# Paired PSUM copies, a later load behind the output weights, and semaphores that make GpSimd wait for VectorE: one change to a fused attention and feed-forward kernel

## The chip, the cores and the metric

The kernel runs on one core of a Trainium2 chip. The metric is the device time of one execution in microseconds (us). Each measured run comes with the mean clock that the throttle granted to TensorE, as a share of full speed. One of the first runs of the kernel before, 280.04 us, was slow and is left out.

Engines have short names in the traces: PE is TensorE, PEld its weight loads, DVE is VectorE, ACT is ScalarE, POOL is GpSimd, SP is SyncE.

## The reference

Attention with a causal local band of 96 keys, 8 global keys and a linear distance bias, over 4 batches, 8 heads, 768 positions and head size 64; then RMS norm and a SwiGLU feed-forward layer on the 3072 resulting rows.

```python
scores = scale * np.matmul(q, k.transpose(0, 1, 3, 2)) + bias      # kept: global or local keys only
a = softmax(scores);  x = np.matmul(a, v)                          # (4, 8, 768, 64) -> (3072, 512)
xn = x / np.sqrt(np.mean(x * x, axis=-1, keepdims=True) + 1e-06) * rms_g
g = xn @ w_gate;  val = xn @ w_val                                 # 512 -> 1536
out = (g * sigmoid(g) * val) @ w_out                               # 1536 -> 512
```

## The kernel before

The work is cut into 8 chunks of 384 rows (half a batch each). A chunk goes through transposes of q and k on TensorE (chunks 0 to 2; later ones use DMA transposes), scores, exponential on ScalarE, masks on VectorE and GpSimd, the product with v, the norm, and then 12 pairs of gate and value products and an output product. TensorE works on the feed-forward part of one chunk while the attention of the next is prepared. So the first feed-forward product of chunk 1 needs, ahead of it, the output product of chunk 0, the norm of chunk 1 and the transposes of chunk 2 that have been placed there.

The order of instructions on each engine comes from a planner in the kernel file. It lists operations with an estimated duration and dependences, simulates the engines, and searches 200 random shifts of priority for the shortest plan. That is why any change of a duration or a dependence gives a new order everywhere.

```python
def tr(c, p, name):                       # transposes of one pair of heads into PSUM
    t = ps_m.tile([128, HB, 128], BF16, tag="m", name="trp")
    ...
def cp(c, p, name, eng):                  # and its copy to SBUF, 128 x 384
    copy(eng)(T[name, c][:, p]..., T["tr", c, p, name]...)

def load_w(what, s):                      # 3 parts each of w_gate, w_val, w_out, issued by GpSimd
    nc.gpsimd.dma_start(w_out[:, ds(4 * s, 4), :], ...)

def glob_v(b, lo, hi):                    # "global copy": values of the 8 global keys, 8 x 1040
    nc.vector.tensor_copy(VG[b % 2][0:NG, lo - 1:hi - 1], _brd(V1[b % 2][0:NG, 0], 1, hi - lo))

def rstd(c):                              # the norm's power, on GpSimd
    nc.gpsimd.tensor_tensor(r, T["ssq", c], half_c, op=ALU.pow)

def fu(c, f):                             # u, on VectorE: its end frees a PSUM bank of the gate product
    nc.vector.scalar_tensor_tensor(u, T["t", c, f], 1.0, T["g", c, f][:, 0:CH], ...)

def kg(c, eng):                           # kG: k again with the 8 global keys put into each block
    copy(eng)(t[:, 0:n], k[:, 0:n])
    ...
def gate(what):                           # a tiny GpSimd copy that makes a later load wait
    ...
    elif what == "v2":                    # v of chunk 2 waits for the last w_val
        src, dst = w_val[0:1, 0, DF - 1:DF], t[0:1, 0, 0:1]
# cut: scores, exponentials, masks, norm, feed-forward, planner, the list of operations
```

The softmax here doesn't subtract the row's maximum and nothing guards it: scores larger than these inputs give would overflow.

Of the kernel before, what the change touches and what calls it, by code (L numbers as in the profile page):

```python
# [39 lines left out]
class _Plan:  # L40
# [11 lines left out]
    START = {"SP": 0.7, "ACT": 0.7, "POOL": 1.9}  # L52
    LAG = {"PE": 0.2, "ACT": 0.1, "DVE": 0.1, "POOL": 0.12, "SP": 0.0}

    def __init__(self, sizes, free):
        self.sizes = sizes
        self.order, self.ops = {}, []
        self.first = dict(free)

# [25 lines left out]
    def _start(self, o, eng):  # L85

        t = max(0.8 if o.kb and eng == "ACT" else self.free[eng], o.at[eng])
        if self._shares(o, eng):
            t = max(t, self.port + (0.15 if eng == "DVE" and self.holder == "POOL" else 0.0))
        if o.kb and eng == "POOL" and len(self.sent) >= 8:  # L90
            t = max(t, self.sent[-8].done)
        need = {}
        for b in o.take:
            need[b.ring] = need.get(b.ring, 0) + 1
        for r, k in need.items():
            used, size = self.rings[r], self.sizes[r]
            if r not in self.LOOSE and any(b not in self.queue[r][:k] for b in o.take if b.ring == r):
                return None
            for i in range(len(used), len(used) + k):
                if i >= size:  # L100
                    old = used[i - size]
                    if old.left:
                        return None
                    t = max(t, old.free)
        return t
# [41 lines left out]
    def search(self, tries, keys, spread):  # L147

        rnd, best, shift = random.Random(6), math.inf, {}
        groups = sorted({key for o in self.ops for key in keys(o)}, key=str)  # L150
        for k in range(tries):
            new = dict(shift)
            if k:
                part = rnd.choice((0.05, 0.2, 1.0))
                amp = rnd.choice(spread)
                for g in groups:
                    if rnd.random() < part:
                        new[g] = new.get(g, 0.0) + rnd.uniform(-amp, amp)
            for o in self.ops:
                o.shift = sum(new.get(g, 0.0) for g in keys(o))  # L160
            end = self.run(call=False)
            if end <= best:
                best, shift = end, new
        for o in self.ops:
            o.shift = sum(shift.get(g, 0.0) for g in keys(o))
        self.run()

    def run(self, slack=0.08, call=True):
# [4 lines left out]
        self.port, self.holder, self.sent, self.issue = 0.0, None, [], 0.0  # L173
# [13 lines left out]
        while left:  # L187
# [25 lines left out]
            if o.kb and eng == "POOL":  # L213
                self.issue = t + dur
            elif eng == "DVE" and t < self.issue and o.fn.__name__ in self.SLOW:
                dur += 0.2
# [24 lines left out]
            if call:  # L241
                o.fn(*o.args, *([] if o.only else [eng]))
# [4 lines left out]
def kernel(  # L247
# [77 lines left out]
    def load_heads(c, name):  # L325

        t = cast_tile(c, name).rearrange("x (h i d) -> x h i d", h=H, i=HB)
        src = {"q": q, "k": k}[name][c // 2, :, ds(CH * (c % 2), CH)]
        nc.gpsimd.dma_start(t.rearrange("x h i d -> x h (i d)"), src.rearrange("h (x i) d -> x h (i d)", i=HB))
# [20 lines left out]
    def load_w(what, s):  # L350
        if what == "o":
            nc.gpsimd.dma_start(w_out[:, ds(4 * s, 4), :],
                                moe_w_out[ds(512 * s, 512)].rearrange("(f p) c -> p f c", p=128))
        else:
            src, t = (moe_w_gate, w_gate) if what == "g" else (moe_w_val, w_val)
            nc.gpsimd.dma_start(t[:, :, ds(512 * s, 512)],
                                src[:, ds(512 * s, 512)].rearrange("(c p) f -> p c f", p=128))
# [99 lines left out]
    def tr(c, p, name):  # L457
        t = ps_m.tile([128, HB, 128], BF16, tag="m", name="trp")
        src = T[name + "b", c]
        for i in range(HB):  # L460
            if c == 0:
                nc.tensor.transpose(t[:, i], src[:, ds(DM * i + 128 * p, 128)], ident)
                continue
            for h in range(2):
                nc.tensor.transpose(t[ds(64 * h, 64), i], src[:, ds(D * (HB * (2 * p + h) + i), D)], ident)  # L465
        T["tr", c, p, name] = t

    def cp(c, p, name, eng):
        if (name, c) not in T:
            T[name, c] = qkp.tile([128, HP, CH], BF16, tag=f"{name}T", name=f"{name}T", bufs=2)  # L470
        copy(eng)(T[name, c][:, p].rearrange("x (t i) -> x t i", i=HB),
                  T["tr", c, p, name].rearrange("x i t -> x t i"))

    def cast_block(c, name, i):
        t = cast_tile(c, name)[:, ds(DM * i, DM)].rearrange("x (h d) -> x h d", h=H)
        nc.gpsimd.tensor_copy(t, T["s" + name, c, i])  # L476
# [13 lines left out]
    def cast_v(c, i, eng="POOL"):  # L490
        b, half = divmod(c, 2)
        J = HB * half + i
        copy(eng)(V1[b % 2][:, J, :, 0:D], T["sv", c, i])  # L493

    def copy_vg(c, i, eng="POOL"):
        b, half = divmod(c, 2)
        J = HB * half + i
        copy(eng)(VG[b % 2][:, J - 1], V1[b % 2][:, J])

    def glob_v(b, lo, hi):  # L500
        nc.vector.tensor_copy(VG[b % 2][0:NG, lo - 1:hi - 1], _brd(V1[b % 2][0:NG, 0], 1, hi - lo))  # L501
# [43 lines left out]
    def kg(c, eng):  # L545
        half = c % 2
        n = HB - half
        t = kg_tile(c)
        k = T["k", c].rearrange("x g (i t) -> x i g t", t=128) if c < NE else T["k", c]
        copy(eng)(t[:, 0:n], k[:, 0:n])  # L550
        lo = 1 - half
        copy(eng)(t[:, lo:n, :, 0:NG], _brd(kg_tile(c - half)[:, 0, :, 0:NG], 1, n - lo))

    def mask(c, p, d, eng):
        half = c % 2
        P = T["P", c, p, d]
        if d == 0:
            m = m00[:, ds(2 * p, 2)] if half == 0 else _brd(_brd(md0, 1, HB), 1, 2)
            nc.vector.tensor_tensor(P, P, m, op=ALU.mult)
        else:  # L560
            lo = 1 if half == 0 else 0
            tt = nc.vector.tensor_tensor if eng == "DVE" else nc.gpsimd.tensor_tensor
            tt(P[:, :, lo:HB, :], P[:, :, lo:HB, :],  # L563
# [45 lines left out]
    def rstd(c):  # L609
        r = xp.tile([128, HB], F32, tag="r", name="r")  # L610
        if c >= NX:
            nc.gpsimd.tensor_scalar(T["ssq", c], T["ssq", c], 1e-6, None, op0=ALU.add)
        nc.gpsimd.tensor_tensor(r, T["ssq", c], half_c, op=ALU.pow)
        T["r", c] = r

    def xn(c, i, eng="DVE"):
# [3 lines left out]
        if c >= NX:  # L620
            e = nc.vector if eng == "DVE" else nc.gpsimd
            e.scalar_tensor_tensor(o, x, r, grow, op0=ALU.mult, op1=ALU.mult)
        elif eng == "ACT":
            nc.scalar.activation(o, x, AF.Copy, scale=r)  # L624
        else:
            nc.vector.tensor_scalar(o, x, r, None, op0=ALU.mult)
# [73 lines left out]
    def gate(what):  # L700
# [5 lines left out]
        elif what == "v2":  # L706
            t = T["gate", 2, "v"] = stg.tile([128, H, D], F32, tag="sv", name="sv")
            src, dst = w_val[0:1, 0, DF - 1:DF], t[0:1, 0, 0:1]
# [3 lines left out]
        nc.gpsimd.tensor_copy(dst, src)  # L712
# [32 lines left out]
    def weights(what, s, due, deps):  # L745
        w_ops[what, s] = add("POOL", 0.8, due, load_w, what, s, deps=deps, kb=2.53, packet=96)
# [3 lines left out]
    def early_part(c):  # L750
# [8 lines left out]
        def load_v():  # L759
            for i in range(HB):  # L760
                sb = buf("sv")
                if c == 2 and i == 0:
                    gated.append(add("POOL", 0.15, START, gate, "v2", deps=[w_ops["v", 2]], take=[sb]))
# [39 lines left out]
        glob[c] = add("DVE", 0.41, due, glob_v, b, lo, hi, deps=gs + old)  # L803
        kg_due = due
        for p in range(HP):
            v_ops[p] = vs + [glob[c]] + old
            due = (START + 8 * p, S1 + 2 * p, S2 + 4 * p)[c]
            for name, ops in (("q", q_ops), ("k", k_ops)):
                t = buf("m")
                o = add("PE", (0.42, 0.36, 0.2)[c], due, tr, c, p, name, deps=[ld[name, p][0], const_ops["ident"]] + hold.get(c, []),  # L810
                        take=[t], give=[ld[name, p][1]])
                tk = [] if p else [(qT_buf if name == "q" else kT_buf)[c]]
                ops[c, p] = [add({"ACT": 0.5} if c == 1 else {"ACT": 0.5, "DVE": 0.5}, 0, due + 1, cp, c, p, name, deps=[o],
                                 give=[t], take=tk)]
        if c >= NK:
            kG_buf[c] = buf("kG", HP + 1 + HP)
            o = add({"DVE": 0.56, "POOL": 1.05}, 0, kg_due + 2, kg, c, deps=[x for p in range(HP) for x in k_ops[c, p]],
                    take=[kG_buf[c]], give=[kT_buf[c]])
# [4 lines left out]
    def sequence_part(c):  # L823
# [44 lines left out]
        glob[c] = add("DVE", 0.35, a0 - 1, glob_v, b, lo, hi, deps=gs)  # L868
# [4 lines left out]
    def attention(c, q_ops, k_ops, v_ops):  # L873
# [6 lines left out]
        for p in range(HP):  # L880
# [3 lines left out]
            if c:  # L884
# [4 lines left out]
                else:  # L889
                    kgd, kgb = [kg_ops[c, p]], [kG_buf[c]]  # L890
                    if half:
                        kgd, kgb = kgd + [kg_ops[c - 1, p]], kgb + [kG_buf[c - 1]]
                o = add("PE", 0.58 if c >= NK else 0.75, a + 2, qk, c, p, 2, take=bufs[0] + bufs[1],
# [27 lines left out]
            o = add("PE", 0.4 if c else 0.57, a + 7, av, c, p, deps=masks + v_ops[p], take=[ab], give=Ps)  # L921
# [20 lines left out]
        if c < NX:  # L942
            t = [buf("m", 2), buf("m", 2)]
            if c == 0:
                pad = add("PE", 1.75, a + 3.9, idle, c, deps=norms, take=t)
            o = [add("PE", 0.25, a + 4, xtr, c, i, deps=[x[i]] + ([pad] if c == 0 else []), take=[] if i or c == 0 else t, give=[xnb])
# [62 lines left out]
    load_g = add("SP", 0.5, START - 40, load_grow, kb=0.7, packet=40, deps=[seq_ops["ld", 1, "v", HB - 1]])  # L1009
    for _ in attention(1, *parts[1]):  # L1010
        pass
    for c in range(2, NCH):
        ops = early_part(c) if c < NE else sequence_part(c)
        for _ in attention(c, *ops):
# [12 lines left out]

    plan.search(TRIES, keys, (1.0, 3.0, 8.0))
# [34 lines left out]
```

## Time and profile before

| | kernel before |
|---|---|
| fast runs of the first rounds | 254.01, 253.53, 253.81 us |
| the profiled run | 251.78 us, clock 1.000, span in the trace 250.0 us |
| first feed-forward product of chunk 0 / of chunk 1 | 26.12 / 55.84 us |
| TensorE's last product ends | 246.29 us |

From the profile page of the kernel before: the line of busy times (engine, busy us, share, instructions), and the load of the output weights (queue, count, size of one, median us from issue to landing).

```profile
PE 232.5 (93%) x1952; PEld 133.2 (53%) x1952; DVE 182.5 (73%) x392; ACT 154.4 (62%) x359; POOL 109.1 (44%) x143
...
w_out<-in_moe_w_out_dram POOLq DMA_DIRECT2D x3, 512.0 KB, 20.7
```

TensorE works almost all the time, so only its idle time can be won. A transfer of output weights takes 20.7 us to land. From 26.1 to 56 us the DMA engines move 204 GB/s at a share of 1.24; at that rate its 512 KB alone would take 2.6 us, so by this estimate most of the 20.7 us is the time of other data. What TensorE waited for, in the same kernel (engine, line and instruction, what it waited for; total us, times, longest):

```profile
PE trp L462 <- DVE qb L333: 8.7, 4, 6.7
...
PE xtp L633 <- DVE xn L626: 1.1, 1, 1.1
PE trp L465 <- DMA kb<-in_k_dram: 0.3, 1, 0.3
```

The first line is mostly the start, before there is any data. The left-out line is the wait of 2.4 us that the prediction shows in its timeline.

### The profile page before, as it was taken

To read this page: it belongs to the slowest core of one execution; us is meant where nothing else is said; L and a number is where in the kernel's file an instruction comes from. 1 tells how busy PE (TensorE), PEld (TensorE's weight loads), DVE (VectorE), ACT (ScalarE), POOL (GpSimd) and SP (SyncE) were. 2 spreads that over 40 slices of the span, in tenths; PEclk is the share of its full clock that TensorE was granted. 3 is DMA by queue.
4 is the path that set the end of the run, shared out by engine and by line. 5 is a ranking of instruction groups with operands and counts; after the bars stand their busy time and mean duration, and the time that the engine had idled before them with its cause. 6 is when DMAs were issued, how large, how long until landed. Compare 5 with 4: busy or idle time off the path is not lost.

```text
span 250.0 us, 5245 instructions
## 1 busy us (share of the span) xinstructions
PE 232.5 (93%) x1952; PEld 133.2 (53%) x1952; DVE 182.5 (73%) x392; ACT 154.4 (62%) x359; POOL 109.1 (44%) x143
## 2 busy tenths in 40 slices
PE   0688879989999999999999999999999999999993
PEld 0346445645555555655655655565555555555541
DVE  6796598878796878998698859887976787545700
ACT  7787746977869879866863695548753444323321
POOL 4094942368939947735576468334420010000000
PEclk9999999999999999999999999999999999999999
DMA  6999999999999669917688759920311014100122
GB/s 172 268 197 205 207 206 194 187 227 220 229 215 201 148 154 221 174 35 177 146 172 167 172 122 171 198 79 29 79 45 42 0 43 107 43 38 7 42 84 84
DMA packets 93353, 34.42 MB, mean 138 GB/s; under 512 B 83472, under 2 KB 90128, under 8 KB 93328
## 3 DMA queue, kind: packets, MB, share of 16 engines
q1 hardware_dynamic: 84144, 27.60, 51.3%
q0 software_dynamic: 8912, 6.29, 16.6%
q8 instruction: 15, 0.25, 0.4%
q10 hardware_dynamic: 272, 0.20, 0.2%
q14 instruction: 10, 0.08, 0.1%
HBM read 28.58 MB, written 6.29 MB: 139 GB/s over the span
## 4 chain that ended last, share of the span: by engine, by line
PE 81%; DVE 5%; DMA 4%; SPq 3%; POOL 2%; ACT 1%; issue 1%; DVEq 0%; ACTq 0%
PE ops L685 24%; PE gps L655 24%; PE vps L662 23%; PE sc L517 4%; DMA kb<-in_k_dram 2%; PE avp L574 2%; PE avp L578 2%; DMA sk<-in_k_dram 2%; SPq L322 2%; DVE VG L501 1%; DVE u L673 1%; PE trp L465 1%; DVE hb L680 1%; PE xtp L633 1%; ACT xn L624 1%
## 5 line engine op out<-in xcount | busy, mean ns | idle before, releaser
L655 PE MATMUL gps<-xT,w_gate 128*128 128x384 bf16 x384 | 78.5, 326 | 0.0
L662 PE MATMUL vps<-xT,w_val 128*128 128x384 bf16 x384 | 78.1, 326 | 0.0
L673 DVE SCALAR_TENSOR_TENSOR u<-t,gps 128x384 f32<-128x384 f32 x96 | 52.9, 551 | 24.1 <-ACT t L668 21.6
L531 ACT ACTIVATE P<-sc,bias 128x384 bf16<-128x384 f32 (+1 forms) x128 | 64.0, 554 | 9.4 <-PE sc L517 5.4
L668 ACT ACTIVATE t<-gps 128x384 f32<-128x384 f32 x96 | 47.0, 490 | 33.1 <-PE gps L655 31.4
L685 PE MATMUL ops<-w_out,hb 128*128 128x512 bf16 x288 | 65.6, 379 | 0.0
L680 DVE TENSOR_TENSOR hb<-u,vps 128x384 bf16<-128x384 f32 x96 | 53.2, 554 | 10.0 <-PE sc L517 0.5
L563 POOL TENSOR_TENSOR P<-P,md 128x768 bf16<-128x768 bf16 (+1 forms) x28 | 42.3, 1509 | 37.6 <-ACT P L531 37.4
L662 PEld LDWEIGHTS <-w_val 128*128 128x128 bf16 x384 | 36.7, 98 | 24.1 <-issue 0.2
L655 PEld LDWEIGHTS <-w_gate 128*128 128x128 bf16 x384 | 35.5, 98 | 23.4 <-issue 0.2
L685 PEld LDWEIGHTS <-hb 128*128 128x128 bf16 x288 | 27.6, 98 | 31.2
L692 ACT ACTIVATE osb<-ops 128x512 f32<-128x512 f32 x23 | 13.7, 597 | 39.5 <-PE ops L685 39.5
L587 DVE TENSOR_TENSOR xu<-avp,rc 128x384 bf16<-128x384 f32 x32 | 17.8, 558 | 1.1
L517 PE MATMUL sc<-qT,kT 64*128 64x128 bf16 x232 | 14.6, 231 | 2.9 <-DVE u L673 2.4
L600 ACT ACTIVATE junk<-xu 128x512 bf16<-128x512 bf16 (+2 forms) x30 | 15.2, 508 | 3.0 <-DVE xu L587 2.2
L493 POOL CAST V<-sv 128x512 bf16<-128x512 f32 x21 | 13.3, 638 | 7.3 <-DMA sv<-in_v_dram 7.2
L574 PE MATMUL avp<-V,P 128*128 128x65 bf16 x192 | 16.3, 200 | 0.0
L574 PEld LDWEIGHTS <-P 128*128 128x128 bf16 x192 | 13.5, 101 | 4.1 <-DVE xu L587 0.5
L476 POOL CAST qb<-sq 128x512 bf16<-128x512 f32 x15 | 9.6, 643 | 8.7 <-DMA sq<-in_q_dram 8.7
L578 PE MATMUL avp<-VG,P 128*128 128x65 bf16 x128 | 12.4, 197 | 0.0
L578 PEld LDWEIGHTS <-P 128*128 128x128 bf16 x160 | 11.5, 100 | 1.0
L517 PEld LDWEIGHTS <-kT 64*128 64x128 bf16 x232 | 8.2, 98 | 6.4 <-issue 4.8
(91 smaller groups left out, 185.9 us busy)
## 6 DMA issues: line engine op xcount, KB each, us to landing
sv<-in_v_dram SPq DMA_DIRECT2D x24, 256.0 KB, 5.0
out_dram<-osb SPq DMA_DIRECT2D x24, 256.0 KB, 2.2
sq<-in_q_dram SPq DMA_DIRECT2D x15, 256.0 KB, 4.5
sk<-in_k_dram SPq DMA_DIRECT2D x15, 256.0 KB, 4.8
w_gate<-in_moe_w_gate_dram POOLq DMA_DIRECT2D x3, 512.0 KB, 12.8
w_val<-in_moe_w_val_dram POOLq DMA_DIRECT2D x3, 512.0 KB, 14.6
w_out<-in_moe_w_out_dram POOLq DMA_DIRECT2D x3, 512.0 KB, 20.7
sq<-in_q_dram SPq DMA_DIRECT2D x4, 192.0 KB, 4.1
```

The source lines that it names most:

```text
L517: nc.tensor.matmul(sc[hh][:, ts(i, 128)], kT[r], qT[r], start=True, stop=True)
L531: nc.scalar.activation(T["P", c, p, d][:, hh, lo:HB, :], T["sc", c, p, d][hh][:, ds(128 * lo, CH - 128 * lo)], AF.Exp, bias=(bias1 if d el ...
L563: tt(P[:, :, lo:HB, :], P[:, :, lo:HB, :], _brd(md1[:, ds(2 * p, 2)], 2, HB - lo), op=ALU.mult)
L574: nc.tensor.matmul(o[:, i, hh, :], P0[:, hh, i, :], V1[b % 2][:, I, h, :], start=True, stop=(I == 0))
L578: nc.tensor.matmul(o[:, i, hh, :], P1[:, hh, i, :], vg, start=False, stop=True)
L587: nc.vector.tensor_tensor(T["xu", c][:, :, ds(2 * p, 2), :], o[:, :, :, 0:64], _brd(rc, 3, 64), op=ALU.mult)
L655: nc.tensor.matmul(g[:, 0:CH], w_gate[:, cc, ts(f, 128)], T["xT", c][:, :, cc], start=(cc == 0), stop=(cc == CC - 1))
L662: nc.tensor.matmul(g[:, 0:CH], w_val[:, cc, ts(f, 128)], T["xT", c][:, :, cc], start=(cc == 0), stop=(cc == CC - 1))
L668: nc.scalar.activation(t, T["g", c, f][:, 0:CH], AF.Tanh, scale=0.5)
L673: nc.vector.scalar_tensor_tensor(u, T["t", c, f], 1.0, T["g", c, f][:, 0:CH], op0=ALU.add, op1=ALU.mult)
L680: nc.vector.tensor_tensor(T["h", c][:, f, :], T["u", c, f], T["v", c, f][:, 0:CH], op=ALU.mult)
L685: nc.tensor.matmul(o, T["h", c][:, f, ts(j, 128)], w_out[:, f, :], start=(f == 0), stop=(f == FC - 1))
```

## The change

The intent: fewer, larger copies of transposed q and k in chunks 1 and 2; v of chunk 2 and the norm weights loaded later, so that the last output weights and q and k of chunk 2 land earlier; no more collisions of VectorE and GpSimd (in the profile before, a copy of VectorE took 2.75 us beside a DMA issue and a mask of GpSimd, where its median is 0.41), by making GpSimd wait on a semaphore; and planner durations nearer to the trace, with a new random seed.

```diff
+    ORDERED = ("mask", "xn", "glob_v", "kg")           # GpSimd's next instruction waits for these
+                if eng == "DVE" and o.fn.__name__ in self.ORDERED:
+                    self.last = ins[1]
+                elif eng == "POOL" and self.last is not None and ins[0] is not None:
+                    self.follow(ins[0], self.last)       # adds the semaphore
-        rnd, best, shift = random.Random(6), math.inf, {}
+        rnd, best, shift = random.Random(3), math.inf, {}
     def tr(c, p, name):
-        t = ps_m.tile([128, HB, 128], BF16, tag="m", name="trp")
+        n = 2 if c else 1
+        t = ps_m.tile([128, n, HB, 128], BF16, tag="m", name="trp")
     def cp(c, p, name, eng):
-        copy(eng)(T[name, c][:, p].rearrange("x (t i) -> x t i", i=HB),
+        copy(eng)(T[name, c][:, ds(p, 2 if c else 1)].rearrange("x g (t i) -> x g t i", i=HB),
-    def glob_v(b, lo, hi):
+    def glob_v(b, lo, hi, eng):                         # VectorE or GpSimd, as the planner likes
         elif what == "v2":
-            src, dst = w_val[0:1, 0, DF - 1:DF], t[0:1, 0, 0:1]
+            src, dst = w_out[0:1, FC - 1, DM - 1:DM], t[0:1, 0, 0:1]
-    load_g = add("SP", 0.5, START - 40, load_grow, ..., deps=[seq_ops["ld", 1, "v", HB - 1]])
+            load_g = add("SP", 0.5, START, load_grow, ..., deps=[seq_ops["ld", 2, "v", HB - 1]])
# cut: return values for the semaphores, planner durations, buffer counts
```

## The prediction

> **What bounds the kernel now.** I began with the page's busy table and its slices: TensorE works 232.5 of the span's 250.0 us, at the full granted clock. So the time is TensorE's work plus TensorE's holes, and the first question is where the 17.5 us of holes lie. Busy time by engine in five stretches (columns: stretch, length, then busy us and instruction count of PE, PEld, DVE, ACT, POOL, then clock, DMA share, GB/s) answers it:
>
> ```profile
> 0.00:6.67 6.67, 0.00 (x1) 0.01 (x1) 4.15 (x24) 5.36 (x19) 2.55 (x15) 1.00 0.71 181
> 6.67:26.10 19.43, 15.40 (x194) 10.37 (x194) 14.48 (x43) 15.24 (x40) 10.16 (x14) 1.00 1.30 220
> 26.10:56.00 29.90, 26.86 (x273) 15.64 (x270) 23.62 (x49) 21.17 (x49) 16.27 (x21) 1.00 1.24 204
> 56.00:246.00 190.00, 190.00 (x1490) 107.22 (x1488) 140.29 (x277) 111.98 (x253) 80.15 (x93) 1.00 0.55 119
> ```
>
> TensorE idles 6.67 us before its first transpose, 4.0 us in the attention of chunk 0, 3.0 us between 26 and 56 us, nothing at all from 56 to 246 us, and some 3.7 us at the end (last eviction and store). Only the 7 us between 6.67 and 56 us are within reach of this change; whatever it does to waits after 56 us is worth nothing unless it opens a hole there.
>
> The timeline of 29 to 34 us then shows the largest single hole (columns: start, duration, engine, line, instruction; in brackets the idle time and its releaser):
>
> ```profile
> 29.66 0.88 POOL L329 DMA_DIRECT2D qb<-in_q_dram  x1
> 29.74 2.75 DVE L501 COPY VG<-V 8x1040 bf16<-8x1040 bf16 x1 [0.78 <-POOL VG L498]
> ...
> 30.56 1.64 POOL L563 TENSOR_TENSOR P<-P,md 128x768 bf16<-128x768 bf16 x1
> 32.42 0.54 DVE L673 SCALAR_TENSOR_TENSOR u<-t,gps 128x384 f32<-128x384 f32 x1
> 33.01 0.33 PE L517 MATMUL sc<-qT,kT 64*128 64x128 bf16 x5 [2.41 <-DVE u L673]
> ```
>
> VectorE's little copy of the global keys' values (L501) took 2.75 us, because GpSimd was issuing a DMA and then masking; the u behind it could not free its PSUM bank, and TensorE stood for 2.41 us. The eight instances of that line say what it should cost:
>
> ```profile
> L501 DVE COPY VG<-V x8: 411/412/2751, 10.4 to 162.6; 8x1040 bf16<-8x1040 bf16 x8
> ```
>
> So 2.75 - 0.41 = 2.34 us of VectorE's time is the collision. The chain of waits agrees: it runs through this copy, u and the scores at 29.7 to 33.6 us, and from 42 to 51 us mostly through VectorE (busy 16.6 of the 18.8 us from 32.5 to 51.3), so VectorE never makes up the loss.
>
> [...]2.75 against 0.41 us, and the mask beside it kept its 1.64 us, so it was VectorE that lost. [...]ScalarE's exponential takes 473 ns at 256 columns and 580 at 384, so 0.84 ns a column and a fixed part of some 260 ns. [...]204 to 220 GB/s with a share above 1 from 6.67 to 56 us[...].
>
> **The change part by part.**
>
> [...]A GpSimd instruction that follows a VectorE mask, xn, kg or global copy now waits for it by semaphore;[...] the global copy may go to GpSimd (planned at 1.25 us). The 2.34 us should vanish, and all of it is on the path: expected -2.3 us. In return GpSimd waits. In chunk 0 there are eight masks of 0.42 to 0.56 us on VectorE from 11 to 20 us, just when GpSimd issues ten DMAs; at worst each delays an issue by half a microsecond, and the DMA engines have a backlog of tens of us (w_out lands 20.7 us after issue), so most of it is hidden. Only the first two issues, k and q of chunk 1 (6.1 and 7.0 us to landing), are nearly on the path. I charge +0.3 us.
>
> The copies two pairs at a time. Chunks 1 and 2 have 16 copies of 128x384 (ScalarE 480 ns, 0.40 start to start in pairs; VectorE 555 ns). Doubled they should cost 480 + 384 x 0.84 = 0.80 us on ScalarE, some 0.72 start to start, so about 0.1 us saved for each of 8: 0.8 us in all. TensorE's 96 transposes stay. Chunk 1's copies run on ScalarE from 19.4 to 25 us beside the squares that the first norm waits for, so part helps there; but a pair's scores now wait for two pairs' transposes. I count -0.1 us.
>
> The DMA order. The 256 KB load of the norm weights was issued at 11.8 us, just ahead of k of chunk 1, and is first used at 127 us; it moves behind chunk 2's v. At about 200 GB/s (estimate from the stretch) it took 1.3 us of the engines. Chunk 1's k landed 6.1 us after its issue and TensorE took it at 18.81 us, with 0.34 us of hole; the chain of waits passes through it, then all 24 transposes, then the last attention product of chunk 0 at 20.23. That product's mask was done at 19.75, so at most 0.5 us of the gain reaches the norm: -0.4 us. The loads of v of chunk 2 (three of 256 KB, issued 37.5 us) now wait for the last w_out, not the last w_val. The last w_out, issued at 27.2 and 20.1 to 21.6 us to landing, is there at 47.3 to 48.8, and its first product runs at 49.9; without this move a TensorE that is 2.3 us early would find it missing. 0.79 MB at 200 GB/s would bring it some 4 us forward. So this part gains little by itself: it lets the 2.3 us through. v is used only at 61.5 us, so it can bear being later.
>
> The new order. Durations closer to the trace (pad 1.1 against 1.0 measured), another seed. Holes of 0.22 and 0.34 us near 54 us, and half of chunk 0's small ones, are its field: -0.4 us, give or take one.
>
> Sum: -2.3 + 0.3 - 0.1 - 0.4 - 0.4 = -2.9 us. The two fast runs before are 254.01 and 253.53, mean 253.8 (the 280.04 I take for a slow one), which gives about **250.9 us**.
>
> **The rivals.** First, the wait changes sides: GpSimd's added waits delay its masks, and the attention product with them. For it: from 60 to 100 us GpSimd is busy 29.1 of 40 us, and a mask takes 1.1 to 1.7 us. Against: it idled 37.4 us before masks waiting for ScalarE, and TensorE has enough other work after 56 us. It would cost 0 to 2 us: 251 to 253. Second, VectorE or ScalarE bounds the stretch from 33 to 51 us anyway, or the DMA backlog (q of chunk 2 landed at 52.5) holds chunk 2: then perhaps 1 us of the 2.3 arrives, 252.5. Speaking for it, VectorE was at 88% there; against it, that work itself begins earlier. Third, the new order fills nearly all the holes: 4 to 4.5 us, about 249.5. A hole that the new order opens after 56 us would make it 254 or more; nothing in the profile points to one.
>
> **Range and chances.** The firm part is 2.3 us; the rest is about 1.5 us either way, so 249.2 to 252.9 should hold it 8 times in 10. Two per cent is 5.1 us, below 248.7, over 70% of all holes within reach: 7%. Slower by 2% needs new holes of 5 us: 2%. Within 2%: 91%.
>
> **What would show it.** Right: no global copy far above 0.42 us on VectorE (or some near 1.25 on GpSimd), no hole of TensorE above 1.3 us after 26 us, idle from 26 to 56 us near 0.5 us, the last w_out landed by 45 us, doubled copies near 0.8 us, chunk 1's k landing sooner after its issue, TensorE's busy time near 232. Wrong: another hole in place of the 2.41 us one, holes after 56 us with masks of GpSimd behind them, a first feed-forward matmul later than 26.1 us, or VectorE's collisions only moved.

## The result, and the profile after

The changed kernel took 250.19, 249.6, 249.95 and 251.13 us, median 250.07, with clocks from 0.997 to 1.000. Executions over 1.5% slower than the fastest of the same kernel are left out of the means. Ratios in this document are the mean time of one kernel's runs over that of the other's runs of the same rounds, so not quite the ratio of the medians; the means of all runs of a batch give the same within 0.001. Here it is 0.9859, with a 95% interval from 0.9819 to 0.990. Repeated later on another chip, with five rounds, the ratio was 0.9914 (0.987 to 0.9957). In the form of the prediction: within 2%, and inside the range, at both times.

Busy time by engine in the stretches that the prediction uses, now of the changed kernel (stretch, length; busy us and instructions of PE, PEld, DVE, ACT, POOL; clock, DMA share, GB/s):

```profile
0.00:6.67 6.67, 1.26 (x11) 0.97 (x12) 4.57 (x26) 5.28 (x19) 2.40 (x15) 1.00 0.77 183
6.67:26.10 19.43, 14.90 (x179) 10.54 (x178) 14.09 (x47) 13.19 (x29) 10.86 (x16) 1.00 1.22 203
26.10:56.00 29.90, 28.75 (x290) 16.93 (x289) 22.29 (x51) 22.67 (x48) 17.91 (x23) 1.00 1.26 212
56.00:246.00 190.00, 188.27 (x1478) 106.32 (x1476) 132.94 (x268) 112.16 (x253) 79.33 (x98) 1.00 0.57 120
```

TensorE idles 1.15 us from 26.1 to 56 us, against 3.04 before. It starts 1.3 us earlier (its first transpose is at 5.37 us) but loses that again before 26.1 us: the first feed-forward product of chunk 0 is at 26.48 us, 0.36 later than before. The 1.7 us of idle time in the last long stretch is the end: the last product ends at 244.27 us. The first feed-forward product of chunk 1 is at 53.79 us, 2.05 earlier than before, and from there to the end of TensorE's last product both traces count the same 190.5 us. So the gain in these two traces is all made before chunk 1's feed-forward part. (In the trace of the repeat, after_again, that product comes still earlier, at 52.97 us, but the rest takes 191.8 us.)

What TensorE waited for in the changed kernel:

```profile
PE trp L478 <- DVE qb L346: 5.9, 2, 5.4
PE trp L481 <- DMA kb<-in_k_dram: 1.2, 1, 1.2
PE sc L534 <- DVE P L580: 0.9, 1, 0.9
PE sc L534 <- DVE kT L560: 0.7, 1, 0.7
```

The 2.4 us behind u are gone, and no hole after 26 us is above 0.6 us. The global copies of the changed kernel by engine (count; min/median/max ns, first to last start):

```profile
L518 DVE COPY VG<-V x6: 411/420/843, 12.0 to 110.9; 8x1040 bf16<-8x1040 bf16 x6
L518 POOL COPY VG<-V x2: 1040/1042/1044, 138.7 to 155.5; 8x1040 bf16<-8x1040 bf16 x2
```

The longest takes 0.84 us where one took 2.75. But the collision has not gone: in the changed kernel the copy of chunk 1 stands two pairs of u and hb (the product behind u) later on VectorE, and it still meets the same mask of GpSimd. The repeat, after_again, shows it more clearly. VectorE's timeline there, and then GpSimd's of the same kernel:

```profile
31.01 1.42 DVE L518 COPY VG<-V 8x1040 bf16<-8x1040 bf16 x1
```

```profile
30.48 1.65 POOL L580 TENSOR_TENSOR P<-P,md 128x768 bf16<-128x768 bf16 x1
```

It takes 1.42 us here, and TensorE has no hole behind it in either trace. So the loss became shorter, and it fell on a place where no product waits for it. On the changed kernel's page the output weights land a little sooner:

```profile
w_out<-in_moe_w_out_dram POOLq DMA_DIRECT2D x3, 512.0 KB, 19.5
```

And GpSimd's timeline from 40 to 52.5 us in the changed kernel (start, duration; in brackets idle time and its releaser):

```profile
44.72 0.18 POOL L730 CAST sv<-w_out 1x1 f32<-1x1 bf16 x1 [3.17 <-DVE rc L603]
46.28 0.88 POOL L630 TENSOR_TENSOR r<-ssq,half_c 128x3 f32<-128x3 f32 x1 [1.38 <-DVE ssq L623]
```

The gate behind the last output weights could read them at 44.72 us, and the power r of chunk 1's norm runs at 46.28 us; before, it ran at 51.04. By the trace the expected thing happened. Whether it happened for the expected reason is what the experiments ask.

### The profile page after: what moved, and what is told of

Same layout as the page of the kernel before. It is cut to its first block, busy times and chain, and to the rows that moved or that the text cites.

```text
span 248.5 us, 5257 instructions
## 1 busy us (share of the span) xinstructions
PE 233.2 (94%) x1952; PEld 134.7 (54%) x1952; DVE 173.9 (70%) x389; ACT 153.3 (62%) x347; POOL 110.5 (44%) x150
## 4 chain that ended last, share of the span: by engine, by line
PE 87%; DMA 4%; DVE 3%; SPq 2%; ACT 1%; POOL 1%; issue 1%; DVEq 0%; ACTq 0%; POOLq 0%
PE ops L703 25%; PE gps L673 25%; PE vps L680 24%; PE sc L534 5%; PE avp L591 2%; DMA kb<-in_k_dram 2%; DMA sv<-in_v_dram 2%; PE avp L595 2%; PE trp L481 2%; SPq L335 1%; PE xtp L651 1%; PE xtp L465 1%; SPq L356 1%; ACT xn L642 1%; DVE xu L604 0%
## 5 line engine op out<-in xcount | busy, mean ns | idle before, releaser
L580 POOL TENSOR_TENSOR P<-P,md 128x768 bf16<-128x768 bf16 (+1 forms) x28 | 40.1, 1431 | 30.7 <-ACT P L548 19.9
L710 ACT ACTIVATE osb<-ops 128x512 f32<-128x512 f32 x22 | 13.1, 597 | 40.4 <-PE ops L703 40.4
L510 POOL CAST V<-sv 128x512 bf16<-128x512 f32 x22 | 14.1, 645 | 14.5 <-DMA sv<-in_v_dram 11.2
L603 DVE RECIPROCAL rc<-avp 128x6 f32<-128x6 f32 x32 | 6.1, 189 | 9.3 <-PE avp L595 9.3
```

What stands on the lines that cost most here:

```text
L580: return tt(P[:, :, lo:HB, :], P[:, :, lo:HB, :], _brd(md1[:, ds(2 * p, 2)], 2, HB - lo), op=ALU.mult)
```

## The experiments

All had five rounds (six runs with the profiled one), in four batches on four chips; the kernel before ran 11 times in each. One of before_sem1's six runs, 255.56 us, was slow and is left out. Names that begin with "before" are edits of the kernel before, with its order of instructions kept; "after" is the changed kernel with its order kept. The last two columns are from the trace of the profiled run.

| run | mean us | ratio to before (95%) | clocks of its runs | first feed-forward product of chunk 0 / chunk 1 | last product ends |
|---|---|---|---|---|---|
| before, profile | | | 1.000 | 26.12 / 55.84 | 246.29 |
| after, profile | 250.22 | 0.9859 (0.9819–0.990) | 0.997–1.000 | 26.48 / 53.79 | 244.27 |
| after_again | 250.48 | 0.9914 (0.987–0.9957) | 0.997–1.000 | 25.60 / 52.97 | 244.75 |
| before_actglob | 253.45 | 1.0031 (0.9981–1.0082) | 0.992–1.000 | 27.80 / 56.6 | 249.14 |
| before_sem1 | 253.32 | 1.0017 (0.9957–1.0076) | 0.992–1.000 | 26.88 / 56.4 | 248.76 |
| after_nosem | 250.94 | 0.9932 (0.9887–0.9977) | 0.999–1.000 | 25.30 / 52.69 | 246.09 |
| before_dma | 253.69 | 1.0005 (0.9957–1.0054) | 0.987–0.998 | 25.78 / 58.88 | 249.15 |
| before_dma_glob | 253.47 | 1.0005 (0.9952–1.0058) | 0.987–0.993 | 25.70 / 56.07 | 247.83 |
| after_early | 253.46 | 1.0004 (0.9963–1.0045) | 0.991–0.993 | 26.41 / 56.9 | 247.39 |
| after_split | 250.10 | 0.9871 (0.983–0.9912) | 0.998–1.000 | 25.88 / 53.24 | 244.25 |
| before_fill | 253.41 | 0.9993 (0.9959–1.0028) | 0.997–1.000 | 27.10 / 56.2 | 247.80 |
| after_collide | 253.76 | 1.0006 (0.9975–1.0037) | 0.992–0.999 | 26.09 / 57.76 | 248.24 |
| after_kfirst | 253.59 | 0.9999 (0.9973–1.0026) | 0.997–1.000 | 25.86 / 54.97 | 248.19 |
| before_three | 252.21 | 0.9971 (0.9921–1.0021) | 0.999–1.000 | 26.38 / 53.47 | 246.14 |

The traces do not begin alike. In before_actglob, before_sem1 and before_fill nothing is edited ahead of chunk 0's first feed-forward product, and yet it comes 0.76 to 1.68 us later than in the profile of the kernel before: TensorE waits 1.05 to 1.78 us for k of chunk 1 there, and 0.34 us in that profile. So look at the distance between the two products, not at the second alone.

**My theory at first** was that of the prediction: the collision of the global copy is the 2.3 us. **The rival**: other limits of nearly the same length lie beside it, so that removing it alone gives little.

**The repeat.** after_again is the changed kernel as it is.

> The changed kernel once more, in the same rounds as the others: 250.1 us, ratio 0.986 to the kernel before. It also tells whether the profile's difference of 1.5 us in span or the timed difference of 3.7 us is the usual one: if the timed 253.8 of the kernel before is steady, the ratio stays at 0.986; if the profiled 251.78 is as frequent, it goes to 0.99.

It took 250.48 us on average where the kernel before took 252.75 on the same chip. The gain is real and this batch puts it at 2.3 us.

**The collision alone, by another engine.** In the kernel before, the one global copy that collided goes to ScalarE, behind the third tanh.

```diff
-        nc.vector.tensor_copy(VG[b % 2][0:NG, lo - 1:hi - 1], _brd(V1[b % 2][0:NG, 0], 1, hi - lo))
+        copy("ACT" if b == 0 and lo == 3 else "DVE")(VG[b % 2][0:NG, lo - 1:hi - 1], ...)
```

> The kernel before in its own order, with one instruction moved: the global copy of chunk 1 (2.75 us on VectorE beside GpSimd) runs on ScalarE[...] behind the third tanh of chunk 0. My theory (the collision is on the path): its 2.3 us come off in full, 251.5 us against 253.8, and the 2.41 us hole of TensorE near 30 us is gone. Rival (VectorE and the DMA backlog bound the stretch to 51 us anyway): at most 1 us, 252.8 or more, with new holes between 42 and 56 us.

The collision is gone and so is its hole, but the time is not lower. TensorE's timeline of before_actglob from 50 to 56 us:

```profile
49.83 1.89 PE L692 MATMUL ops<-w_out,hb 128*128 128x512 bf16 x8
53.67 0.36 PE L472 MATMUL trp<-ident,qb 128*64 128x128 bf16 x6 [1.95 <-DMA qb<-in_q_dram]
```

TensorE reaches the transposes of chunk 2 earlier and then stands 1.95 us for q of chunk 2. The hole has moved 21 us down the line. And a second one opens near 88 us, where the kernel before's profile has none. VectorE's timeline from 80 to 90 us in before_actglob, and then TensorE's of the same kernel:

```profile
85.55 1.85 DVE L508 COPY VG<-V 8x1040 bf16<-8x1040 bf16 x1
```

```profile
88.16 0.20 PE L581 MATMUL avp<-V,P 128*128 128x65 bf16 x1 [1.38 <-DVE xu L594]
```

There another global copy, which took 0.41 us in that profile, falls beside a mask of GpSimd (84.67 to 87.12 us) and takes 1.85 us. This run missed my theory's expectation, 251.5.

**The collision alone, by one semaphore.** In the kernel before, GpSimd's first mask of chunk 1 waits for the global copy, in the changed kernel's own way. (The edit does the same once in each batch.)

```diff
+                if o.fn.__name__ == "glob_v" and o.args[1] == 3:
+                    self.last = ins
+                elif eng == "POOL" and self.last is not None and ins is not None:
+                    self.follow(ins, self.last)
```

> The kernel before in its own order, with one semaphore added: GpSimd's first mask of chunk 1 waits for VectorE's global copy of chunk 1. The DMA issue ahead of that mask still meets the copy, so the copy should last about 1.3 us instead of 2.75. Theory: 1.2 to 1.5 us come off, 252.3 to 252.6 us. Rival (the late mask gives the time back): no change, 253.8.

What TensorE of before_sem1 waited for:

```profile
PE trp L471 <- DMA qb<-in_q_dram: 2.3, 1, 2.3
```

It is the same wait, and again there is no gain; the hole near 88 us is there too, 1.34 us. The copy took 0.41 us, not the 1.3 that I expected: this time the DMA issue, which had begun 0.02 us before it, did not make it longer. Two different ways of removing the collision agree, so the 2.34 us is not worth 2.34 us by itself.

**The loads alone.** In the kernel before, v of chunk 2 and its gate go behind the last output weights, and the norm weights behind v.

```diff
+                if name == "load_grow" or not flushed and (o.args == ("v2",) or
+                        name == "load_block" and o.args[:2] == (2, "v")):
+                    held.append(o); continue        # issued behind the last GpSimd mask of chunk 1
-            src, dst = w_val[0:1, 0, DF - 1:DF], t[0:1, 0, 0:1]
+            src, dst = w_out[0:1, FC - 1, DM - 1:DM], t[0:1, 0, 0:1]
```

> The kernel before in its own order, with the DMA order of the change alone: the gate and the three loads of v of chunk 2 wait for the last output weights, the norm weights load behind them; VectorE's slow global copy stays. New theory (two serial limits stand side by side, the collision and the landing of q of chunk 2; taking either alone brings little): within 0.7 us of the kernel before at the same granted clock, so 251 to 251.7 us in runs at a clock of 0.997 or more, and about 253.5 in runs at 0.993, if there are any; the hole of 2.4 us at 30 us stays. Rival (the loads alone were what the change gained): 250.3 to 250.6.

There is no gain here either: the collision's hole is still there. What TensorE of before_dma waited for, and then the clock in 40 slices from its page, in tenths:

```profile
PE sc L529 <- DVE u L685: 2.6, 1, 2.6
```

```profile
PEclk9999959999999999999999999999999999999999
```

The second view shows something that the kernel before's own profile had not: in the slice from 31.6 to 37.9 us, where this hole of 2.56 us ends, the granted clock is about half (0.50 from 33 to 39 us in stretches of 1 and 2 us).

**Both together.** before_dma_glob has both edits.

> The kernel before in its own order, with the DMA order of the change and the global copy of chunk 1 on ScalarE. New theory (the two limits together): 249.8 to 250.6 us, no TensorE hole above 1.3 us after 26 us, no run with a clock of 0.993. Rival (the gain lies in the new order or in the doubled copies): 251.5 us or more at full clock, as with the copy moved alone.

This missed too: 253.47 us. GpSimd's timeline of before_dma_glob, and then ScalarE's of the same kernel:

```profile
50.19 0.61 POOL L508 CAST V<-sv 128x512 bf16<-128x512 f32 x1 [3.31 <-DMA sv<-in_v_dram]
...
50.89 0.89 POOL L628 TENSOR_TENSOR r<-ssq,half_c 128x3 f32<-128x3 f32 x1
```

```profile
51.80 1.95 ACT L639 ACTIVATE xn<-xu,r 128x512 bf16<-128x512 bf16 x3 [3.96 <-POOL r L628]
```

The load of v is later now, as it should be; but in the old order GpSimd's cast of that v stands ahead of the norm's power r, and r began at 50.89 us, right behind it. So r waits for a load that it does not need, and TensorE stands 2.68 us for the normed rows. It is a third limit, and this one belongs to the order.

**All three.** before_three is before_dma_glob with the cast of v behind r.

```diff
+                if name == "cast_v" and o.args == (2, 0):
+                    vcast = o; continue
                 o.fn(*o.args, *([] if o.only else [eng]))
+                if name == "rstd" and o.args == (1,):
+                    vcast.fn(*vcast.args, "POOL")
```

> The kernel before in its own order with three repairs: the DMA order of the change, the global copy of chunk 1 on ScalarE, and on GpSimd the first cast of v of chunk 2 behind the power of chunk 1's norm instead of ahead of it (there it held the norm from 47.9 to 50.9 us). Theory (three limits of nearly the same length stand one behind the other; each alone is worth nothing, all three together the whole): the TensorE hole of 2.7 us before chunk 1's transposes goes, chunk 1's first feed-forward product comes near 53 us instead of 56, ratio 0.986 to 0.992 to the kernel before, all runs at a mean clock of 0.997 or more. Rival (a fourth limit, in the order of chunk 1's attention or of chunk 2): ratio above 0.996.

Now chunk 1's feed-forward part begins at 53.47 us, as early as in the changed kernel, and no hole above 0.34 us is left between 26 and 56 us. But TensorE's last product ends at 246.14 us, where it ended before. The timeline of before_three near 70 us:

```profile
69.92 0.43 DVE L570 COPY kG<-kT 128x1024 bf16<-128x1024 bf16 x1 [1.35 <-DMA kT<-kb]
70.39 0.18 DVE L572 COPY kG<-kG 128x64 bf16<-128x64 bf16 x1
...
70.62 0.29 PE L537 MATMUL sc<-qT,kG 64*128 64x128 bf16 x4 [1.10 <-DVE kG L572]
```

A TensorE that is 2 us early meets the transposed k of chunk 3, which comes by DMA, and stands 1.10 us for the copy behind it. All idle time from 56 to 100 us is 1.84 us. That is a fourth limit. The changed kernel's profile does not show it, with 190.48 us from chunk 1's first feed-forward product to the end of the last product, against 192.67 here. But the new order is not free of it: where it came to this point early it stood before the same product, 0.85 us at 70.92 us in after_nosem and 0.90 us at 73.41 us in after_kfirst. Compared with the kernel before's runs at a clock of 0.997 or more on that chip (five, mean 251.98), 252.21 is no gain; the 0.8 us below the mean of all its runs is that none of before_three's runs lost its clock.

**The collision put back into the changed kernel.** after_collide emits the global copy right behind the copies it depends on, without a semaphore.

```diff
+                if name == "glob_v" and o.args[:3] == (0, 3, 5):
+                    continue
+                if name == "copy_vg" and o.args[:2] == (1, 1):
+                    self.early()                      # glob_v(0, 3, 5, "DVE")
```

> The changed kernel in its own order, with the collision put back: VectorE's global copy of chunk 1 goes one place pair earlier, so that it meets GpSimd's DMA issue and mask at 30 us without a semaphore. Theory (all three parts are needed: DMA order, place of the copy, order of chunk 1's attention): the copy takes 2.3 us or more, a TensorE hole of 1.5 to 2.4 us opens near 31 us, 252 to 254 us. Rival (with the other parts in place the collision is absorbed): within 0.5 us of the changed kernel, 250.5.

The whole gain is lost. VectorE's timeline of after_collide, and then TensorE's of the same kernel:

```profile
29.80 2.73 DVE L523 COPY VG<-V 8x1040 bf16<-8x1040 bf16 x1 [0.87 <-POOL VG L520]
32.47 0.53 DVE L696 SCALAR_TENSOR_TENSOR u<-t,gps 128x384 f32<-128x384 f32 x1
```

```profile
33.05 0.32 PE L539 MATMUL sc<-qT,kT 64*128 64x128 bf16 x5 [2.48 <-DVE u L696]
```

The loss is made up of the hole of 2.48 us and of a stretch of half clock behind it, which the part on the clock shows. So the copy in this place costs all of the gain when the rest of the change is there; when it is not, taking the copy away brings nothing.

**The old loads in the changed kernel.** after_early keeps the new order but issues v of chunk 2, gated on the last w_val, behind the second GpSimd mask of chunk 1, and the norm weights behind v of chunk 1.

```diff
+                if name == "mask" and o.args == (1, 1, 1, "POOL"):
+                    more = [gate "v2"] + [the three loads of v of chunk 2]
+                if name == "load_block" and o.args == (1, "v", 2):
+                    more = [load_grow]
-            src, dst = w_out[0:1, FC - 1, DM - 1:DM], t[0:1, 0, 0:1]
+            src, dst = w_val[0:1, 0, DF - 1:DF], t[0:1, 0, 0:1]
```

> The changed kernel in its own order, with the old DMA order: gate of v of chunk 2 on the last w_val, behind the second mask of chunk 1, norm weights right behind v of chunk 1. New theory: k and q of chunk 2 land 3 to 4 us later, TensorE waits 2 us or more near 47 to 52 us for them, the clock halves for some 3.5 us behind that hole in most runs; 252.5 to 254.5 us. Rival (the DMA order matters little once the collision is gone): at most 0.7 us above the changed kernel, 251.2.

The whole gain is lost here as well. TensorE's timeline of after_early:

```profile
49.26 1.49 PE L494 MATMUL trp<-ident,kb 128*64 128x128 bf16 x24 [3.22 <-DMA kb<-in_k_dram]
```

TensorE stands 3.22 us for k of chunk 2. The load order is needed in full too. A detail for later: k of chunk 1 was issued at 13.09 us and used at 18.98 us here, 5.89 us, against 13.35 and 19.06, 5.71 us, with the norm weights moved. On these two traces the norm weights are worth 0.2 us.

**The copies of two pairs.** after_split does each doubled copy as two single ones, at the same place.

```diff
+        for g in range(2 if c else 1):
+            copy(eng)(T[name, c][:, ds(p + g, 1)]..., T["tr", c, p, name][:, ds(g, 1)]...)
```

> The changed kernel in its own order, each doubled copy of q and k of chunk 1 and 2 split into two copies of one pair on the same engine. From 0.80 us for a doubled copy and 0.40 start to start for a single one, 0.1 us more for each of 8: if they are off the path, within 0.3 us of the changed kernel; if the doubled copies carry the gain, 1 us or more slower.

It took 250.10 us, as good as the changed kernel's 250.22 and 250.48. The doubled copy takes 0.80 us on ScalarE, as worked out, but nothing on the path needed the time that it saves.

**The semaphores.** after_nosem drops all the added semaphores and keeps the order.

```diff
-    plan.follow = follow
+    plan.follow = lambda ins, other: None
```

> The changed kernel, same order of instructions on every engine, but GpSimd does not wait for VectorE[...] (the waits serve no data). Theory A (the planned order alone keeps the engines apart): within 0.4 us of the changed kernel, about 250.1. Theory B (the semaphores carry the gain): collisions return, a global copy, mask or kG copy on VectorE takes over 1 us between 26 and 56 us, and the time rises by 1 to 2.5 us.

It took 250.94 us against 250.48 for the changed kernel on the same chip, 0.46 more, with intervals of the ratios that overlap. The global copy of chunk 1 took 1.41 us without them, but with them it took 0.84 us in one trace and 1.42 in the other, so they do not keep it from the mask. On the other side, GpSimd's timeline from 10 to 20 us in the changed kernel shows what they cost:

```profile
12.86 0.18 POOL L730 CAST kb<-sk 1x1 bf16<-1x1 f32 x1 [1.18 <-DVE P L580]
13.35 1.13 POOL L342 DMA_DIRECT2D kb<-in_k_dram  x1 [0.31 <-POOL kb L730]
```

GpSimd stands 1.18 us for a mask of VectorE before it may issue k of chunk 1; without semaphores the issue is at 12.79 us, 0.56 earlier, and TensorE has this k 0.45 us earlier. So it is the place of the copy in the new order, not the semaphores, that makes its collision harmless. Whether the semaphores are worth anything elsewhere was not resolved.

**More of the same.** If the landing of k and q of chunk 2 was the next limit, bringing them further forward might give more. after_kfirst issues them ahead of the last output weights.

```diff
+                if name == "load_w" and o.args == ("o", 2) or not flushed and (v of chunk 2, its gate):
+                    held.append(o); continue
+                if name == "load_heads" and o.args == (2, "q"):
+                    held.pop(0)                        # now the last w_out
```

> A version that may beat both: the changed kernel in its own order, but k and q of chunk 2 are issued ahead of the last w_out, and the gate of v of chunk 2 stands behind the first norm of chunk 1. TensorE's hole of 0.6 to 1.7 us before chunk 2's k near 46 us should go, since k lands some 5 us earlier; the last w_out should land near 48.8 us, just before its first product at 50.7. Theory: 249.6 to 250.1 us, 0.4 to 0.8 below the changed kernel. Rival (v of chunk 2 or w_out now comes late): no gain, or a new hole at 50 us and 251 or more.

This was a miss: 253.59 us at full clock. The wait for k of chunk 2 falls away, but the timeline of after_kfirst shows what comes instead:

```profile
52.83 1.46 POOL L580 COPY kG<-kT 128x1536 bf16<-128x1536 bf16 x1
...
54.34 0.53 PE L547 MATMUL sc<-qT,kG 64*128 64x128 bf16 x4 [1.50 <-POOL kG L580]
```

GpSimd first waits 3.22 us for v of chunk 2, which is later now; behind its cast, the copy of chunk 2's k starts only at 52.83 us and ends when TensorE has stood 1.50 us; a hole of 0.90 us near 73 us follows. The load order of the changed kernel lies between two limits.

**The clock.** Is the loss in these runs the hole, or the half clock behind it? before_fill keeps TensorE busy in the kernel before's hole with 36 products whose result nobody uses (in its trace they run from 31.25 to 33.4 us).

```diff
+                if o.fn.__name__ == "qk" and o.args == (1, 1, 2):
+                    self.fill()          # 36 x matmul(t, warm, warm), 128 x 128
```

> The kernel before in its own order, with 36 dummy products of 128x128 on TensorE (2.0 us at full clock, into the free attention bank) exactly where it stands idle at 30.4 to 33.0 us. Theory (the spread of the kernel before, 251.5 at a mean clock near 1.0 and 253.8 at 0.993, comes from a halving of the granted clock for some 3.6 us, set off by this hole): all runs at 0.997 or more and 251.3 to 252.0 us. Rival (the clock falls for another reason, such as the hole near 23 us): the share of runs at 0.993 stays about two thirds and the median at 253.5.

All six runs kept a clock of 0.997 or more, while 6 of the 11 runs of the kernel before on that chip were at 0.993 or below. So the hole does set off the drop, as far as six runs can show it. The time did not follow: 253.41 us, where the kernel before had 253.14 at full clock and 254.08 at the lower one. The filled hole is as long as the empty one, so no more than the clock's share could come back, and that was not resolved. (Its trace loses 0.98 us before chunk 0's first feed-forward product and 1.15 us after chunk 1's against the profile of the kernel before.)

The drop itself is on the page of after_collide (clock in 40 slices of 6.3 us, in tenths):

```profile
PEclk9999979999999999999999999999999999999999
```

The slices mix it with full speed. In stretches of 1 us the clock of before_actglob is 0.50 from 55 to 58 us with parts of that beside, 3.4 us of half clock in all; after_collide and after_early also have 3.4 us, and before_dma's profile, at a mean clock of 0.987, about twice that. At half speed 3.4 us lose 1.7 us, which fits a mean of 0.993 over 250 us. Over the four batches the kernel before had 19 runs at 0.997 or more, mean 252.36 us, and 25 at 0.995 or less, mean 253.86. The drop costs 1.5 us where it comes, and it comes in about half of its executions. The changed kernel had 0.997 or more in all 10 of its runs.

## Why the prediction was right or wrong

The number held: 250.9 predicted, 250.07 and then 250.52 measured as medians. Its sum held less well, point by point.

**TensorE bounds, and only holes before 56 us can be won: right.** The whole gain in the trace, 2.0 us, lies ahead of chunk 1's first feed-forward product, and TensorE's busy time is 233.2 us, against 232.5 before.

**"The 2.34 us should vanish, and all of it is on the path: expected -2.3 us": this step failed as a term of a sum.** The copy's loss did not vanish: it is 0.43 us in one trace and 1.0 us in the repeat, where no product waits for it. The 2.41 us hole did vanish, and the trace's gain between the first feed-forward products of chunk 0 and chunk 1 is 2.41 us, which looks like a proof. But removing the collision alone gained nothing (before_actglob 1.0031, before_sem1 1.0017), while putting it back lost everything (after_collide 1.0006). The profile before already showed why. TensorE's timeline there, and then GpSimd's of the same kernel:

```profile
52.59 0.36 PE L465 MATMUL trp<-ident,qb 128*64 128x128 bf16 x6
52.88 0.87 PE L633 MATMUL xtp<-ident,xn 128*128 128x128 bf16 x8
```

```profile
51.04 0.88 POOL L613 TENSOR_TENSOR r<-ssq,half_c 128x3 f32<-128x3 f32 x1 [2.72 <-DVE ssq L606]
```

TensorE comes to the transposes of chunk 2's q at 52.59 us with no wait. That q was issued at 29.66 and took 22.8 us, so it landed at about 52.5: it was just in time. Transposes of the normed rows follow at 52.88, from an r that ended at 51.92. No wait is shown, because the hole at 30 us had already used up the slack; take it away, and they become the waits of 1.95, 2.3 and 2.68 us that the runs show. In before_actglob and before_sem1 the collision of a later copy came on top, with 1.38 and 1.34 us. These are limits of almost equal length side by side, and time comes only when all of them move. In the changed kernel they all do. The same timeline of TensorE in the changed kernel:

```profile
49.91 0.86 PE L481 MATMUL trp<-ident,qb 128*64 128x128 bf16 x24
50.70 2.76 PE L703 MATMUL ops<-w_out,hb 128*128 128x512 bf16 x12
...
53.79 0.82 PE L673 MATMUL gps<-xT,w_gate 128*128 128x384 bf16 x4
```

Chunk 2's q, issued at 29.85, lands after 18.9 us, about 48.75, nearly 4 us sooner, and its transposes run ahead of the output product.

**"So this part gains little by itself: it lets the 2.3 us through": right**, and shown from both sides (before_dma 1.0005, after_early 1.0004). The prediction named the last output weights as what would be missing. In the runs it was q or k of chunk 2, issued in the same queue. The second rival named q of chunk 2 and guessed that 1 us of 2.3 would arrive without more; nothing measurable arrived.

**The term of 0.4 us for the new order was the mis-sized one.** The order is needed for everything: with loads and copy moved but the old order kept, GpSimd's cast stood ahead of r (before_dma_glob; the prediction said that v is used only at 61.5 us and can be late, but this cast reads it at 47.53 us in the profile before); with that mended, a copy near 70 us gave the gain back (before_three).

**Norm weights and chunk 1's k, -0.4: open.** Between the two profiles it did not arrive: the landing is 5.57 us from issue instead of 6.10, but the issue is 0.8 us later. The first feed-forward product was one of my signs of failure, "later than 26.1": it is at 26.48. But the profile before was a lucky execution here. In three others with the same order and the same loads up to this point (before_actglob, before_sem1, before_fill) TensorE took this k at 19.57 to 20.49 us and began chunk 0's feed-forward part at 26.88 to 27.80. In the three with only the norm weights moved up to this point (before_dma, before_dma_glob, before_three) it was 18.38 to 19.06 and 25.70 to 26.38 us. That speaks for about 1 us, after_early's 0.2 us speaks against it, and the traces come from different chips. **GpSimd's waits, +0.3:** of the right size, 0.45 us at this k. **Doubled copies, -0.1:** no effect shown.

**The base.** I subtracted from 253.8 us, a mean of timed runs, terms read from a trace whose execution took 251.78. Between the two profiled executions the gain is 251.78 to 250.19, 1.6 us. On one chip at a clock of 0.997 or more it is 252.03 to 250.48, also 1.6 us, out of 2.3 us between all runs there. The rest is the clock drop that the kernel before suffers in part of its executions and the changed kernel in none. The prediction didn't have this term, and it made up for what the others lacked: that the sum met the timed result so closely was luck. For the first rounds, where the mean difference is 3.6 us, the clocks of the timed runs before were not recorded, so that share is argued, not shown.

Other signs that I named: the idle time from 26 to 56 us was to be near 0.5 us and is 1.15; a global copy far above 0.42 us on VectorE was to be absent, and there is one of 0.84 us, in the repeat of 1.42; the global copy on GpSimd was to be near 1.25 us and takes 1.04; the last output weights had landed by 44.72 us, as said.

**What stays open.** Whether the new order is good for its better durations or by the luck of its seed was not separated. The spread of the kernel before at full clock (251.3 to 254.3 us) is explained at most in part: the 1.7 us by which the traces with its order differ at chunk 0's first feed-forward product go with the landing of chunk 1's k. Nor is it known what exactly sets off the clock drop. No run beat the changed kernel; after_split equals it.

## What to carry to other kernels

A hole in the busiest engine hides whatever is only just in time behind it, so before counting a hole as gain, look at how late each of the next inputs (loads, normed rows, copies) arrives where that engine would be early. Removing one limit alone and finding nothing does not show that it was harmless: put it back into the finished version as well. Look at more than one trace of a kernel before saying that a loss has gone. And compare the profiled execution's time with the timed runs before subtracting one from the other.

## What the traces show of the clock and of the collision

- In the profiled runs the granted clock fell to 0.50 at holes of 1.95 us (before_actglob), 2.3 us (before_sem1), 2.48 us (after_collide), 2.56 us (before_dma) and 3.22 us (after_early). At the hole of 2.68 us in before_dma_glob the run's mean clock was 0.993, and the four gate products that came first took 1.46 us together, where four take 0.82 later in the same trace. Behind 26 us it did not fall after holes up to 1.66 us (after_nosem), nor in the profile of the kernel before after 2.41 us. The low stretch lasted 3.4 us in before_actglob, after_collide and after_early, and 6.8 us in before_dma. So the length of the hole alone does not tell, in these traces, whether the clock falls.
- The global copy was longer than its 0.41 us beside two instructions of GpSimd in a row: begun at 29.74 us, during a DMA issue of GpSimd that ended at 30.54, it did not end before a mask that began 0.02 us after that issue; it took 2.75 us in all, and after_collide repeated it with 2.73. In both, and in the six traces of the new order where it began beside the mask alone, it ended 0.28 to 0.30 us behind the mask. A DMA issue does not always go with a longer copy: in before_sem1 a copy begun 0.02 us into one took 0.41 us. Why the copy takes longer there was not shown; the traces give the times only.
